# Attention and gated feed-forward: score runs of a key block in pairs, from batch 4 on

## The chip, the cores and the metric

The kernel runs on one core of a Trainium2 chip. The metric is the device time of one launch in microseconds, the median of the runs. Profiled numbers come from one execution on the same core.

## What is computed

For 8 batches of 8 heads, 576 positions and 64 dimensions: causal attention with a decay bias, then over all 4608 tokens a feed-forward layer with root-mean-square normalisation and a SiLU gate (512 to 1536 to 512).

```python
scores = scale * np.matmul(q, k.transpose(0, 1, 3, 2))
cum = np.cumsum(np.maximum(s, 0.0), axis=-1)
bias = -(cum[:, :, :, None] - cum[:, :, None, :])
scores = np.where(causal, -1e9, scores + np.minimum(bias, 0.0))
attn = softmax(scores)                     # over the keys
x = (attn @ v).transpose(0, 2, 1, 3).reshape(4608, 512)
xn = x / np.sqrt(np.mean(x * x, -1) + 1e-6) * rms_g
g = xn @ w_gate
out = (g / (1 + np.exp(-g)) * (xn @ w_val)) @ w_out
```

## The kernel before

The feed-forward runs in nine chunks of 512 tokens (`ffn`). In a chunk, for each of twelve blocks of 128 inner features, four matmuls of 128x512 make the gate (L751) and four the value (L760), each in a bank of the four-bank ring psF. ScalarE takes the tanh T of half the gate (L754), VectorE makes U = (T + 1) x gate (L763), and Ht = U x value (L756). Then four output tiles of twelve matmuls each (L773) are made; ScalarE copies them out as osb (L778).

The attention of later batches is put between these matmuls by a planner that runs while the program is written. `step()` is called 36 times in a chunk, after every block of four feed-forward matmuls or so; `slot[0]` counts the steps. The steps 1 to 24 of a chunk lie in the gate and value part, the rest among the outputs. Each step first issues what is pending from the step before, then may scale an x (`x_scale`) and start its transpose on SP's queue, run one entry of some side queues (casts, loads, magnitude checks), and then `place()` puts at most a score run, or values and transposes, into TensorE's order. A lag such as `ready(5, "S", b, qb, g)` asks that the scores were placed at least five steps ago.

Batch b has five key blocks kb; queries of a key block are the same 128 positions and the next 128. `s_step` (L249) makes the scores of one key block for four heads (g = 0 or 1): four matmuls (L278) that each use half of the rows of the array (64 dimensions), the two halves writing two banks, psS[0] and psS[1]. Four exps follow on ScalarE (L302), the first two at once and the other two in the next step, and then a mask on POOL (L311), into one of eight slots of E. The last key block has 64 positions and one run of eight small matmuls for all heads.

`av_step` (L336) makes the values of 128 queries for four heads: up to eight matmuls of 65 columns (L344, L350) into psAV for g = 0 and into psT for g = 1. VectorE takes the reciprocal of the sums (L357) and writes x_sb (L359). After g = 1, ScalarE takes the sum of squares (L366), POOL makes alpha from it (L379, L382), and `x_scale` (L389) multiplies x by alpha and the weights g_row. `xt_dma` (L400) transposes the result into xnT, which the chunks read; `need(c)` would put warm-up matmuls (L674) where a chunk's x is late.

PSUM has eight banks here: four of psF, two of psS, one of psAV, one of psT.

The rules around the change: a score run waits until the last one is 4, 3 or 2 steps back, by how far ahead of its due step it is; values until the last values are 2 steps back and their scores 5 steps; x is scaled 3 steps after the values of g = 1; the transposes of keys and queries (L182) keep off SP's queue just ahead of an x that is to be scaled. A slot of E is free when its two readers have been placed.

Of the kernel before, what the change touches and what calls it, by code (L numbers as in the profile page):

```python
# [26 lines left out]
def kernel(  # L27
# [13 lines left out]
    B, H, S, D = q.shape  # L41
# [40 lines left out]
    kqTx = kqT.rearrange("d a w (c h n) -> d a w c h n", c=NSC, h=HP)  # L82
    XB = 2
    KB = 4
    v_sb = mp.tile([128, 2, NSC, H, NV], BF16, name="v_sb")

    NE = 8
# [154 lines left out]
    def slot_free():  # L242
        return eread.get(ecount[0] % NE, 0) == 0
# [2 lines left out]
        for ps in pair:  # L246
            nc.tensor.matmul(ps, lhsT=ident_bf, rhs=mneg, start=True, stop=False)

    def s_step(b, kb, g, pair=None, masked=False):  # L249

        p = b % 2
        N = (256, 256, 256, 192, 64)[kb]
        W = 64 if kb == 4 else 256
        nj = 4 if kb == 4 else 2
        e = take_slot((b, kb, g), 2 if kb in (0, 1, 2, 3) else 2)
        if pair is None:
            ps = psS()
            pair = (ps[:, 0, :], ps[:, 1, :])

        wide, premask = b == 0, b == 0 and kb < 4  # L260
        if premask and not masked:
            masks(pair)
        heads = []
        for j in range(nj):
            hp = (0 if kb == 4 else 2 * g) + j
            for par in (0, 1):
                rs = slice(par * 64, par * 64 + 64)
                if b < KB:
                    kT = kqTn[rs, p, 0, hp, kb * 128:kb * 128 + 128]
                else:  # L270
                    kT = kqTx[rs, p, 0, kb, hp, :]
                if b < XB:
                    qT = kqTn[rs, p, 1, hp, kb * 128:kb * 128 + N]
                    M = N
                else:
                    qT = kqTx[rs, p, 1, kb, hp, 0:64] if kb == 4 else kqTx[rs, p, 1, kb:kb + 2, hp, :]
                    M = W
                nc.tensor.matmul(  # L278
                    pair[par][:, j * W:j * W + M], lhsT=kT, rhs=qT,
                    start=(j == 0 and not premask), stop=(j == nj - 1))  # L280
                heads.append((2 * hp + par, par, j * W))
        if kb == 4:
            Ev = E[:, e].rearrange("p h (a n) -> p (h a) n", n=128)
            h0, nh, nq = 0, 8, 64
        else:
            Ev = E[:, e]
            h0, nh, nq = 4 * g, 4, 128

        def exps(part):
            for h, par, o in part:  # L290
                bh = b * H + h
                parts = [(0, N)]
                if b >= XB and kb == 3:
                    parts = [(0, 128), (128, 192)]
                for n0, n1 in parts:
                    eo = Ev[:, h - h0, n0:n1]
                    ei = pair[par][:, o + n0:o + n1]
                    if b >= XB and (n1 - n0) % 128 == 0:

                        eo = eo.rearrange("k (a p r) -> k a p r", p=32, r=4)  # L300
                        ei = ei.rearrange("k (a r p) -> k a p r", p=32, r=4)
                    nc.scalar.activation(out=eo, in_=ei, func=AF.Exp, scale=0.125,  # L302
                                         bias=biasK[:, kb, bh:bh + 1])

        def second(masked=True):
            exps(heads[nj:])
            if masked:
                mask()

        def mask():  # L310
            nc.gpsimd.affine_select(  # L311
                out=Ev[:, :, 0:nq], in_=Ev[:, :, 0:nq],
                pattern=[[0, nh], [1, nq]], compare_op=ALU.is_ge, fill=0.0, base=0,
                channel_multiplier=-1)

        def whole():
            for par in (0, 1):
                nc.scalar.activation(
                    out=Ev.rearrange("k (j a) n -> k a j n", a=2)[:, par, :, 0:N],
                    in_=pair[par][:, 0:nj * W].rearrange("k (j n) -> k j n", j=nj)[:, :, 0:N],  # L320
                    func=AF.Exp, scale=0.125)

        if premask:
            return whole
        if wide:
            whole()
            return mask
        exps(heads[:nj])
        return second

# [103 lines left out]
    slot = [0]  # L434
    first, chunk = [0], [0]
    done = {}
    last = {"S": -9, "AV": -9, "T": -9, "X": -9, "AVT": -9, "L": -9}
    s_seq = [(b, kb, g) for b in range(B) for kb in range(NSC) for g in (0, 1) if kb < 4 or g == 0]
    s_seq.sort(key=lambda x: (1, 0, x[2], x[1]) if x[0] == 1 and x[1] < 2 else (x[0], x[1], x[2], 0))
    av_seq = [(b, qb, g) for b in range(B) for qb in range(NSC) for g in (0, 1)]  # L440
# [9 lines left out]
    def at(*key):  # L450
        return done.get(key, 10 ** 6)
# [30 lines left out]
    def phase():  # L482

        return slot[0] - first[0]
# [86 lines left out]
        done["T", b, hp, w] = slot[0]  # L571
        last["T"] = slot[0]

    def do_s(key, pair=None, masked=False):
        b, kb, g = key
        second = s_step(b, kb, g, pair, masked)
        done["S", b, kb, g] = slot[0]
        if kb == 4:
            done["S", b, 4, 1] = slot[0]
        last["S"] = slot[0]  # L580
        return second
# [23 lines left out]
    def can_t():  # L605
# [10 lines left out]
            return ready(2, "cast", 1, "tail") if hp == "tail" else ready(2, "cast", 1, w, hp // 2)  # L616
        return (ready(2, "cast", b) or ready(2, "cast", b, w)) and (b < 2 or ready(1, "S", b - 2, 4, 0))

    def can_s():
        if not s_seq or not slot_free():  # L620
            return False
        b, kb, g = s_seq[0]
        if b == 1 and (phase() < 24 and phase() % 2 == 0 or kb == 4 and at("AV", 1, 3, 1) > slot[0]):
            return False
        due = SLOTS * ((b * S + kb * 128) // DM) - (26 if b == 1 else 18 if b < 4 else 14)
        if slot[0] - last["S"] < (4 if slot[0] < due - 24 else 3 if slot[0] < due else 2):
            return False
        if b >= XB:
            return all(ready(5, "X", b, 1, c) for c in (kb, min(kb + 1, 4))) and (
                ready(5, "X", b, 0, kb) if b >= KB else ready(3, "T", b) if kb >= 3 else  # L630
                all(ready(3, "T", b, hp, 0) for hp in (2 * g, 2 * g + 1)))
        if kb >= 3 and not ready(3, "T", b):
            return False
        if kb == 4:
            return True
        return all(ready(3, "T", b, 2 * g + j, w) for j in (0, 1) for w in (0, 1))

    def can_av(clear=False):
        if not av_seq:
            return False  # L640
        b, qb, g = av_seq[0]
        if slot[0] - last["AV"] < (1 if (b, qb) == (1, 3) else 2):
            return False
        if b > 0 and g == 1 and slot[0] - last["T"] < 3 and not clear:
            return False
        if b > 1 and not ready(8, "V", b):
            return False
        if qb > 0 and not ready(5, "S", b, qb - 1, g):
            return False
        prev = b * NSC + qb - NX  # L650
        if prev >= 0 and at("XT", prev // NSC, prev % NSC) > slot[0]:
            return False
        return ready(4 if (b, qb) == (1, 3) else 5, "S", b, qb, g)

    def by_pe(b, qb):

# [19 lines left out]
    def step(bare=False):  # L676

        slot[0] += 1
        while pending:
            pending.pop(0)()  # L680
        moved = False
        if scaled[0] < len(x_list):
            b, qb = x_list[scaled[0]]
            if ready(3, "AV", b, qb, 1):
                x_scale(b, qb)
                scaled[0] += 1
                if not by_pe(b, qb):
                    assert xt_seq[0] == (b, qb)
                    xt_dma(*xt_seq.pop(0))
                    done["XT", b, qb] = slot[0] + 4  # L690
                    moved = True
        run_side(act_side)

        if not moved and x_seq and slot[0] - last["X"] >= 2 and not (
                scaled[0] < len(x_list) and x_list[scaled[0]] != (1, 4) and ready(1, "AV", *x_list[scaled[0]], 1)):
            b, w, c = x_seq[0]
            if (ready(1 if b == 2 else 2, "cast", b, 1) and ready(1, "S", b - 2, 4, 0)
                    and (w == 1 or ready(7, "K", b, c))):
                x_seq.pop(0)
                kq_dma(b, w, c)  # L700
                done["X", b, w, c] = last["X"] = slot[0]
                if b >= KB and (w, c) == (0, NSC - 1) and b + 2 < B:
                    casts(b + 2)
        bare = bare or chunk[0] == 0 and 30 <= phase() <= 33
        if slot[0] % 2 and not bare and not (chunk[0] == 0 and phase() >= 24):
            run_side(v_side)
        if not bare:
            run_side(pool_side)
        place()
        run_side(dve_side)  # L710

    def place():

        if can_s():
            pending.append(do_s(s_seq.pop(0)))
            if t_seq and t_seq[0][0] == 1 and can_t():
                do_t(t_seq.pop(0))
            return
# [517 lines left out]
```

## Time and profile before

| | us |
|---|---|
| Runs | 363.77, 365.58, 370.51 |
| Median | 365.58 |
| Profiled execution | 364.69 |
| Span of its profile | 363.0 |
| PE busy | 348.8 (96%) |
| VectorE (DVE) busy | 273.4 (75%) |
| ScalarE (ACT) busy | 239.8 (66%) |
| GpSimd (POOL) busy | 178.2 (49%) |

PE is TensorE's matmuls, PEld its weight loads, SP the queue of the sync engine. In the rows of the profile "L278" is a line of the kernel; a row of the timeline has the start, the time from the first start to the last end, the engine, the line, the operation, the tile written and those read, and how many instructions are merged in it. Ends of matmuls are modelled and matmuls overlap, so the order of their starts tells more than their durations. The granted clock of TensorE was 0.999 over the span.

### The profile page before, as it was taken

Reading aid. Unit: us, or ns where it says so; the run is one execution under the profiler, and the core shown is the slowest. Engines: PE = TensorE matmul, PEld = TensorE weight load, DVE = VectorE, ACT = ScalarE, POOL = GpSimd, SP = SyncE. Lnnn points to the kernel's source line nnn. Section 1 sums busy time; section 2 is a strip of 40 time slices with the busy share of each in tenths; the row PEclk is TensorE's granted clock in tenths of the full one; section 3 lists DMA queues with packets and bytes.
Section 4 is the critical chain, followed back from the end, with each engine's and each line's share of the span. In section 5 each row is a group of like instructions: output and inputs, shape, how many; then the busy total and the mean of one; then the engine's idle time right before and its main releaser. Section 6 shows DMA issues by size and latency. Waiting matters only on the chain. (4 is left out here: it accounts for less than half of the span.)

```text
span 363.0 us, 6976 instructions
## 1 busy us (share of the span) xinstructions
PE 348.8 (96%) x2383; PEld 160.5 (44%) x2383; DVE 273.4 (75%) x523; ACT 239.8 (66%) x619; POOL 178.2 (49%) x283
## 2 busy tenths in 40 slices
PE   4989999999999999999999999999999999999993
PEld 2445444444445444444444444444444444444441
DVE  6697988698888889788998988884588548827820
ACT  3988884768886778877778768776777653223311
POOL 7959765858865566869737954622232200000000
PEclk9999999999999999999999999999999999999999
DMA  7999999999969399969979994973201130020011
GB/s 228 132 229 256 177 170 259 182 201 193 212 127 138 59 198 138 167 147 163 164 202 124 140 142 105 115 85 90 78 14 17 51 103 1 0 88 29 1 60 60
DMA packets 124096, 45.81 MB, mean 126 GB/s; under 512 B 103956, under 2 KB 118808, under 8 KB 124056
## 3 DMA queue, kind: packets, MB, share of 16 engines
q0 software_dynamic: 62688, 14.29, 47.4%
q1 hardware_dynamic: 51872, 23.80, 32.1%
q10 hardware_dynamic: 9496, 7.23, 8.4%
q8 instruction: 19, 0.31, 0.4%
q14 instruction: 21, 0.17, 0.2%
HBM read 37.90 MB, written 9.44 MB: 130 GB/s over the span
## 5 line engine op out<-in xcount | busy, mean ns | idle before, releaser
L302 ACT ACTIVATE E<-psS,biasK 128x256 bf16<-128x256 f32 (+3 forms) x328 | 107.0, 415 | 18.9 <-PE psS L278 18.6
L751 PE MATMUL psF<-xnT,wg_sb 128*128 128x512 bf16 x432 | 111.1, 379 | 0.6 <-ACT xnT L416 0.3
L760 PE MATMUL psF<-xnT,wv_sb 128*128 128x512 bf16 x432 | 111.1, 379 | 0.0
L773 PE MATMUL psF<-wout_sb,Ht 128*128 128x512 bf16 x432 | 102.5, 379 | 0.1
L763 DVE SCALAR_TENSOR_TENSOR U<-T,psF 128x512 bf16<-128x512 f32 x108 | 73.7, 682 | 29.4 <-ACT T L754 29.4
L754 ACT ACTIVATE T<-psF 128x512 f32<-128x512 f32 x108 | 64.4, 596 | 41.0 <-PE psF L751 38.6
L311 POOL TENSOR_SCALAR_AFFINE_SELECT E<-E 128x512 bf16<-128x512 bf16 x64 | 46.5, 727 | 77.5 <-ACT E L302 77.0
L756 DVE TENSOR_TENSOR Ht<-U,psF 128x512 bf16<-128x512 bf16 x99 | 67.7, 684 | 7.0 <-PE psF L760 0.5
L751 PEld LDWEIGHTS <-wg_sb 128*128 128x128 bf16 x432 | 38.7, 98 | 44.9 <-issue 5.6
L773 PEld LDWEIGHTS <-Ht 128*128 128x128 bf16 x432 | 38.6, 97 | 42.4 <-issue 2.3
L760 PEld LDWEIGHTS <-wv_sb 128*128 128x128 bf16 x432 | 38.5, 98 | 42.2 <-issue 4.2
L778 ACT ACTIVATE osb<-psF 128x512 f32<-128x512 f32 x36 | 21.5, 596 | 32.0 <-PE psF L773 25.5
L389 DVE SCALAR_TENSOR_TENSOR xs_sb<-x_sb,al_all,g_row 128x512 bf16<-128x512 bf16 (+1 forms) x36 | 29.9, 831 | 12.8 <-POOL al_all L382 12.1
L186 POOL DMA_DIRECT2D v_sb<-in_v_dram x40 | 35.4, 888 | 0.7 <-PE psAV L350 0.3
L366 ACT ACTIVATE xs_sb<-x_sb 128x512 bf16<-128x512 bf16 (+1 forms) x37 | 23.5, 636 | 17.9 <-DVE x_sb L359 17.5
L427 DVE TENSOR_TENSOR acc<-acc,mag 128x1280 bf16<-128x1280 bf16 x32 | 26.6, 845 | 0.2
L278 PE MATMUL psS<-kqT 64*128 64x256 bf16 (+2 forms) x304 | 25.9, 256 | 0.9 <-ACT kqT L203 0.5
L350 PEld LDWEIGHTS <-E 128*128 128x128 bf16 x320 | 21.7, 98 | 10.0 <-issue 0.2
L379 POOL TENSOR_SCALAR al_all<-ss_all 128x1 f32<-128x1 f32 (+2 forms) x39 | 10.7, 274 | 29.7 <-ACT xs_sb L366 22.9
L382 POOL TENSOR_TENSOR al_all<-al_all,mhalf 128x1 f32<-128x1 f32 (+2 forms) x39 | 22.2, 570 | 3.2
L344 PEld LDWEIGHTS <-E 128*128 128x128 bf16 x256 | 20.0, 98 | 8.6 <-DVE x_sb L359 1.6
L278 PEld LDWEIGHTS <-kqT 64*128 64x128 bf16 x320 | 9.2, 94 | 30.8 <-issue 29.9
(126 smaller groups left out, 301.0 us busy)
## 6 DMA issues: line engine op xcount, KB each, us to landing
out_dram<-osb SPq DMA_DIRECT2D x36, 256.0 KB, 2.3
kq<-in_q_dram ACTq DMA_DIRECT2D x5, 1024.0 KB, 6.2
v_sb<-in_v_dram POOLq DMA_DIRECT2D x32, 128.0 KB, 6.4
kq<-in_k_dram SPq DMA_DIRECT2D x4, 512.0 KB, 5.6
kq<-in_q_dram SPq DMA_DIRECT2D x4, 512.0 KB, 7.5
kqn<-in_k_dram POOLq DMA_DIRECT2D x16, 128.0 KB, 5.4
wout_sb<-in_moe_w_out_dram POOLq DMA_DIRECT2D x2, 768.0 KB, 9.9
kq<-in_q_dram POOLq DMA_DIRECT2D x1, 1024.0 KB, 10.8
```

Of the source, the lines that this page charges most:

```text
L186: nc.gpsimd.dma_start(out=v_sb[0:n, b % 2, c, :, 0:64], in_=v[b, :, c * 128:c * 128 + n, :].rearrange("h p d -> p h d"))
L278: nc.tensor.matmul(pair[par][:, j * W:j * W + M], lhsT=kT, rhs=qT, start=(j == 0 and not premask), stop=(j == nj - 1))
L302: nc.scalar.activation(out=eo, in_=ei, func=AF.Exp, scale=0.125, bias=biasK[:, kb, bh:bh + 1])
L311: nc.gpsimd.affine_select(out=Ev[:, :, 0:nq], in_=Ev[:, :, 0:nq], pattern=[[0, nh], [1, nq]], compare_op=ALU.is_ge, fill=0.0, base=0, chan ...
L389: nc.vector.scalar_tensor_tensor(out=xs_sb[0:n, (b * NSC + qb) % NX, :], in0=x_sb[0:n, (b * NSC + qb) % NX, :], scalar=al_all[0:n, col:col ...
L427: nc.vector.tensor_tensor(out=acc[:, sl], in0=acc[:, sl], in1=mag[:, sl], op=ALU.max)
L751: nc.tensor.matmul(Gp, lhsT=wg_sb[:, cc, fs], rhs=xnT[:, cc, x0:x0 + DM], start=(cc == 0), stop=(cc == CC - 1))
L754: nc.scalar.activation(out=T, in_=Gp, func=AF.Tanh, scale=0.5)
L756: nc.vector.tensor_tensor(out=Ht[:, fb - 1, :], in0=pend[0], in1=pend[1], op=ALU.mult)
L760: nc.tensor.matmul(Vp, lhsT=wv_sb[:, cc, fs], rhs=xnT[:, cc, x0:x0 + DM], start=(cc == 0), stop=(cc == CC - 1))
L763: nc.vector.scalar_tensor_tensor(out=U, in0=T, scalar=1.0, in1=Gp, op0=ALU.add, op1=ALU.mult)
L773: nc.tensor.matmul(Op, lhsT=Ht[:, fb, tb * 128:(tb + 1) * 128], rhs=wout_sb[:, fb, :], start=(fb == 0), stop=(fb == FB - 1))
```

## The change

From batch 4 on (`PB = 4`), and for the four large key blocks, `place()` takes both score runs of a key block in one step. The run of g = 1 comes first and goes to psS; its exps are held. The run of g = 0 follows at once and goes to psAV and psT, the banks of the values. The exps of g = 0 are issued in this step and the next one, those of g = 1 in the two steps after that, so `pending` now holds a step for each entry. A pair waits for the last scores (six steps after the held run, which is counted two steps late; four steps at the first key block), for the last values (two steps) and for two free slots of E; values wait three steps after a pair, since they use its banks. The values of g = 1 may follow those of g = 0 in the next step, four steps after their scores' counted step. From batch 4 on x is scaled five steps behind its values instead of three, and the transposes on SP keep off accordingly. Score runs that are not paired wait three steps from batch 4 on.

```diff
+    PB = 4
...
-    def s_step(b, kb, g, pair=None, masked=False):
+    def s_step(b, kb, g, pair=None, masked=False, hold=False):
...
+        if hold:
+            return lambda: exps(heads[:nj]), second
         exps(heads[:nj])
         return second
...
-    last = {"S": -9, "AV": -9, "T": -9, "X": -9, "AVT": -9, "L": -9}
+    last = {"P": -9, "S": -9, "AV": -9, "T": -9, "X": -9, "AVT": -9, "L": -9}
...
-    def do_s(key, pair=None, masked=False):
+    def do_s(key, pair=None, masked=False, hold=False):
         b, kb, g = key
-        second = s_step(b, kb, g, pair, masked)
+        second = s_step(b, kb, g, pair, masked, hold)
...
+    def paired(key):
+        return key[0] >= PB and key[1] < 4 and key[2] == 0
+
     def can_s():
-        if not s_seq or not slot_free():
+        if not s_seq or not slot_free() or pending:
             return False
         b, kb, g = s_seq[0]
+        if paired(s_seq[0]):
+            if eread.get((ecount[0] + 1) % NE, 0) > 0 or slot[0] - last["AV"] < 2:
+                return False
+            if slot[0] - last["S"] < (6 if kb else 4):
+                return False
...
-        if slot[0] - last["S"] < (4 if slot[0] < due - 24 else 3 if slot[0] < due else 2):
+        if slot[0] - last["S"] < (3 if b >= PB else 4 if slot[0] < due - 24 else 3 if slot[0] < due else 2):
             return False
...
-        if slot[0] - last["AV"] < (1 if (b, qb) == (1, 3) else 2):
+        if slot[0] - last["AV"] < (1 if (b, qb) == (1, 3) or b >= PB and g == 1 else 2):
+            return False
+        if slot[0] - last["P"] < 3:
             return False
...
-        return ready(4 if (b, qb) == (1, 3) else 5, "S", b, qb, g)
+        return ready(4 if (b, qb) == (1, 3) or b >= PB and g == 1 and qb < 4 else 5, "S", b, qb, g)
...
-        while pending:
-            pending.pop(0)()
+        while pending and pending[0][0] <= slot[0]:
+            pending.pop(0)[1]()
...
-            if ready(3, "AV", b, qb, 1):
+            if ready(3 if b < PB else 5, "AV", b, qb, 1):
                 x_scale(b, qb)
...
-                scaled[0] < len(x_list) and x_list[scaled[0]] != (1, 4) and ready(1, "AV", *x_list[scaled[0]], 1)):
+                scaled[0] < len(x_list) and x_list[scaled[0]] != (1, 4) and ready(1 if x_list[scaled[0]][0] < PB else 3, "AV", *x_list[scaled[0]], 1)):
...
         if can_s():
-            pending.append(do_s(s_seq.pop(0)))
+            if paired(s_seq[0]):
+
+                b, kb, g = s_seq.pop(0)
+                first4, last4 = do_s(s_seq.pop(0), hold=True)
+                pair = (psAV(), psT32())
+                pending.extend([(slot[0] + 1, do_s((b, kb, g), pair)),
+                                (slot[0] + 2, first4), (slot[0] + 3, last4)])
+                done["S", b, kb, 1] = slot[0] + 2
+                last["P"], last["S"] = slot[0], slot[0] + 2
+                return
+            pending.append((slot[0] + 1, do_s(s_seq.pop(0))))
```

## The prediction

> **What bounds the kernel now.** I read the page first (busy times, the 40 slices), then the windows of the part in which batches 4 to 7 are scored, then the groups of lines there, then the order of TensorE's work in single steps.
>
> ```profile
> span 363.0 us, 6976 instructions
> PE 348.8 (96%) x2383; PEld 160.5 (44%) x2383; DVE 273.4 (75%) x523; ACT 239.8 (66%) x619; POOL 178.2 (49%) x283
> PE   4989999999999999999999999999999999999993
> ```
>
> ```profile
> 143.50:179.00 35.50, 35.50 (x258) 16.07 (x256) 29.91 (x56) 27.24 (x80) 28.21 (x44) 1.00 1.49 154
> 179.00:214.00 35.00, 35.00 (x248) 15.66 (x247) 31.84 (x61) 26.80 (x75) 22.59 (x35) 1.00 1.32 154
> 214.00:250.00 36.00, 36.00 (x253) 16.14 (x252) 29.46 (x55) 26.32 (x72) 14.89 (x24) 1.00 0.80 104
> 250.00:286.00 36.00, 36.00 (x253) 16.17 (x252) 24.23 (x47) 26.11 (x72) 9.96 (x19) 1.00 0.17 47
> ```
>
> After the stretch's length the columns are PE, PEld, DVE, ACT and POOL busy, the granted clock and DMA. TensorE never idles between 143.5 and 286 us; no other engine is full (DVE at most 31.84 of 35.00). So nothing that only takes load off another engine shortens this part. What can shorten it is time in which TensorE counts as busy and streams nothing. I looked for that around a score run (four score matmuls):
>
> ```profile
> 201.31 1.03 PE L760 MATMUL psF<-xnT,wv_sb 128*128 128x512 bf16 x4
> 202.27 0.39 PE L278 MATMUL psS<-kqT 64*128 64x256 bf16 x4
> 202.60 1.04 PE L751 MATMUL psF<-xnT,wg_sb 128*128 128x512 bf16 x4
> 203.47 0.19 PE L344 MATMUL psT<-v_sb,E 128*128 128x65 bf16 x1
> ...
> 203.71 1.02 PE L760 MATMUL psF<-xnT,wv_sb 128*128 128x512 bf16 x4
> 204.57 1.03 PE L751 MATMUL psF<-xnT,wg_sb 128*128 128x512 bf16 x4
> 205.44 1.03 PE L760 MATMUL psF<-xnT,wv_sb 128*128 128x512 bf16 x4
> ```
>
> ```profile
> L278 PE MATMUL psS<-kqT x304: 190/269/280, 10.5 to 284.7; 64*128 64x256 bf16 x114, 64*128 64x64 bf16 x32, 64*128 64x192 bf16 x6
> ```
>
> Start to start, an undisturbed feed-forward block of four takes 0.86 to 0.87 us (203.71, 204.57, 205.44); I use 0.865. The block before the scores takes 0.96 (201.31 to 202.27), the scores 0.33, the block behind 0.87. A score run therefore costs 0.96 + 0.33 + 0.87 - 2 x 0.865 = **0.43 us**. Inside it little time is streaming: the four records span 0.39 us and one lasts 0.27, so the last starts 0.12 after the first; the two pairs (one matmul on each half of the rows) follow each other at 0.12. Two pairs are 0.24; the other 0.19 is the price of going from full-height matmuls to half-height ones and back.
>
> **The change, part by part.**
>
> *Pairing the score runs.* Batches 4 to 7, key blocks 0 to 3: 16 pairs of runs. Two runs apart cost 0.86. Eight matmuls in a row cost 0.43 + 2 x 0.12 = 0.67, so a pair saves 0.19 and 16 save **3.0 us**. The second four write psAV and psT, which no score run of the trace does, so I bound them: at least the pace of the feed-forward, 512 columns in 0.865/4 = 0.216 us (then 0.21 saved each, 3.4 in all); at most a whole run of 0.43 again (nothing saved). I take 0.24, since they are the same shape behind the same shape, as the second pair of a run is now.
>
> By the Trainium skill (TensorEngine Tiling (Array Packing), Tiling Modes, Key Properties) the array drains when the tiling mode changes and not when only the tile does, which is for 0.24 rather than 0.43; no run here has two score runs in a row.
>
> *The step pattern.* From the rules: pair at step k, its values at k+5 and k+6, the next pair at k+8 (the held run counts as k+2, plus six; the values plus two). By hand the pairs fall on steps 109, 119, 127, 135, 144, 153, 161, 169, 178, 187, 195, 203, 212, 221, 229, 237: about 34 steps for a batch, where the feed-forward supplies 36 x 576/512 = 40.5. Scores end at step 242, the last scaling at 253, of 324 steps; chunk 4, starting at step 144, needs a block scaled at 130, that is 14 x 0.865 = 12 us earlier. So attention is never late for a chunk:
>
> ```profile
> DMA to landing us min/median/max: 2.3/3.7/8.5
> L400 SPq DMA_TRANSPOSE xnT<-xs_sb x34: 1171/1190/1852, 56.5 to 295.5; - x34
> 325.31 1.03 PE L751 MATMUL psF<-xnT,wg_sb 128*128 128x512 bf16 x4
> ```
>
> The last transpose is issued at 295.5 and the last chunk begins at 325.31. Scaling two steps later (1.7 us) costs nothing by this cover; without it, 1.7 us per chunk. SP's queue holds the same transposes, and each waits less for its scaling; the loads keep their order on POOL.
>
> *The exps.* A run's exps now occupy two steps; a pair's occupy four in a row, with the tanhs between, on ScalarE's one queue. Rows for the durations:
>
> ```profile
> 200.04 0.83 ACT L302 ACTIVATE E<-psS,biasK 128x256 bf16<-128x256 f32 x2
> 201.21 0.90 POOL L162 DMA_DIRECT2D kqn<-in_k_dram  x1
> 202.71 1.03 ACT L302 ACTIVATE E<-psS,biasK 128x128 bf16<-128x128 f32 x4 [0.60 <-PE psS L278]
> 203.67 0.60 ACT L754 ACTIVATE T<-psF 128x512 f32<-128x512 f32 x1
> 204.06 0.18 DVE L357 RECIPROCAL rZ<-psT 128x4 f32<-128x4 f32 x1
> 204.16 1.03 ACT L302 ACTIVATE E<-psS,biasK 128x128 bf16<-128x128 f32 x4
> 204.27 0.42 DVE L359 TENSOR_TENSOR x_sb<-psT,rZ 128x256 bf16<-128x256 f32 x1
> 204.61 0.68 DVE L763 SCALAR_TENSOR_TENSOR U<-T,psF 128x512 bf16<-128x512 f32 x1
> 205.06 0.63 POOL L311 TENSOR_SCALAR_AFFINE_SELECT E<-E 128x512 bf16<-128x512 bf16 x1
> 205.64 0.60 POOL L156 CAST kqn<-kq 128x512 bf16<-128x512 f32 x1
> ...
> 207.60 0.19 PE L344 MATMUL psAV<-v_sb,E 128*128 128x65 bf16 x1
> ```
>
> Neighbours on ScalarE overlap by some 0.08 (the exps of 202.71 end at 203.74, the tanh starts at 203.67), so two exps occupy 0.75; a tanh occupies 0.49 (203.67 to 204.16) and starts 0.20 after its block (203.47). Let a pair's first matmul start at 0, in the gate/value part, behind a gate block. TensorE: scores to 0.57, then blocks to 1.44, 2.30, 3.17, 4.03, 4.90; the first values 4.90 to 5.14; a block; the second values at 6.00. ScalarE: exps start 0.44 after the scores (202.27 to 202.71) plus 0.24 = 0.68; the first half-runs end at 1.43 and 2.18; a tanh 2.50 to 3.0; the held half-runs end at 3.75 and 4.50; the next tanh, due at 4.23, starts at 4.50. Its gate bank is wanted only two blocks after the one that follows it, so this delay of 0.27 is hidden.
>
> POOL's masks (0.63) end at 2.8 and 5.1. The first values want theirs at 4.90, the second at 6.00: **0.9 us of cover**, where a run has 1.9 today (scores 202.27, mask over at 205.69, values 207.60). Queued ahead of the held mask are the key and value issues (0.90 each): from 2.8, two of them end at 4.6 and the mask at 5.2, still in time; with a cast (0.60) too the mask ends at 5.8. A mask can also last longer:
>
> ```profile
> L311 POOL TENSOR_SCALAR_AFFINE_SELECT E<-E x64: 624/635/1331, 30.9 to 287.4; 128x512 bf16<-128x512 bf16 x64
> L389 DVE SCALAR_TENSOR_TENSOR xs_sb<-x_sb,al_all,g_row x36: 732/752/1428, 42.2 to 294.1; 128x512 bf16<-128x512 bf16 x28, 64x512 bf16<-64x512 bf16 x8
> ```
>
> The longest took 1.33, 0.70 over the median. In the new order the scaling of x (step k+3 when pairs are eight apart) is issued in the same step as the held mask. With 0.70 more, behind three issues, the mask ends at 6.5: a wait of 0.5. I count one such case in 16, about 0.3 us with smaller ones. Lower bound 0; upper bound every pair, in the rival below.
>
> The Trainium skill (SBUF — State Buffer, Who interferes with whom) has a rule that speaks against the move: a VectorE instruction with two inputs in SBUF and a GpSimd one that reads SBUF exclude each other for a whole instruction. The two maxima above agree in size; by it alone, every pair with a scaling in its mask's step would see that delay, yet only those also behind three issues would wait.
>
> *The banks psAV and psT.* The second four wait for VectorE's reads of the values two steps earlier. These end 0.98 after the values (203.71 to 204.69), so at 6.24 + 0.98 = 7.2; with one Ht or U (0.68) ahead, 7.9. The next pair's second four start at 0.57 + 8 x 0.865 + 2 x 0.24 + 0.10 + 0.24 = 8.3. Covered by 0.4. If it fails, the next thing late is the whole row of eight matmuls and TensorE with it.
>
> **Sum.** The profiled execution took 364.69 us (span 363.0 and 1.69 around it). 364.69 - 3.0 + 0.3 = **362.0 us**. The profiled execution lies 0.89 below the median of the runs shown (365.58), and the fastest run 0.92 below the profiled one (363.77); 362.0 is 1.0% under the median.
>
> **The rivals.**
>
> 1. *Small waits eat half.* VectorE is at 31.84 of 35.00 in its fullest window, so the cover of 0.4 on the banks can fail where pairs follow eight steps apart in the gate/value part. Six do (127, 161, 195, 203, 229, 237); at 0.3 each 1.8 us: 363.5. Against it: the scaling no longer waits for alpha there.
> 2. *The switch is paid again* for the second four because they go to other banks: nothing saved, 364.7. Against it: pairs inside a run already alternate between two banks at 0.12.
> 3. *The held half's mask decides* (slower). If exps do not overlap (0.83 a half-run, tanh 0.60), the held half ends at 0.68 + 1.66 + 0.17 + 0.60 + 1.66 = 4.8; with one issue of 0.90 after that, the mask ends at 6.3, and at 7.0 where it lasts 1.33. TensorE then waits some 0.75 (between 0.3 and 1.0) at the second values. In the 11 pairs of the gate/value part this is 8.3: 364.69 - 3.0 + 8.3 = 370.0. It decides from 0.19 per pair on, a held mask that ends 1.1 us later than I have it. For it: today too POOL waits for exps before anything else. Against it: POOL is busy only 9.96 to 28.21 of some 36 us, and the overlap is in the rows.
>
> **How the numbers follow.** Forecast 0.58 (its own range 361.0 to 363.0), rival 1 0.22, rival 2 0.05, rival 3 0.12, something larger in either direction 0.03. The range goes down to 360.3 (3.4 saved, no waits, and the 0.9 by which the fastest run is under the profiled one) and up to 367.0, which leaves out most of rival 3. A difference under 2% is about what a measurement of this kernel can't tell from none. Faster by over 2% would take 7.3 us, more than twice all that the switches of these runs cost: 0.03. Slower by over 2% means 373 us, rival 3 in every pair: 0.05. Within: 0.92.
>
> **What would show it.** Right: in the changed profile score runs of eight, about 0.57 from first start to the next block; eight steps between them; values in neighbouring steps; PE still full between 143 and 283, that stretch some 3 us shorter; masks of held runs ending before their values. Wrong: idle time of PEld or PE before L344/L350 put to POOL (rival 3) or before L278 put to VectorE (rival 1); a gap of 0.2 inside the row of eight (rival 2); warm-up matmuls (L674) between chunks, which would mean that x came late.

## The result and the profile after

The changed kernel takes 367.45 us (median of 22 runs, 366.21 to 371.65), the kernel before 365.84 (22 runs). The ratio is 1.0063, 95% interval 1.0038 to 1.0088: a small loss, where 362.0, a gain of 1%, was forecast and 367.0 was the upper end of the range. The profiled executions took 366.71 and 364.69, with spans of 365.0 and 363.0.

The change does what it says. In the order of TensorE's work there are score runs of eight, the second four in psAV and psT (the columns are start, time to the last end, engine, line):

```profile
200.40 1.03 PE L783 MATMUL psF<-xnT,wv_sb 128*128 128x512 bf16 x4
201.35 0.39 PE L279 MATMUL psS<-kqT 64*128 64x256 bf16 x4
201.58 0.27 PE L279 MATMUL psAV<-kqT 64*128 64x256 bf16 x1
201.59 0.27 PE L279 MATMUL psT<-kqT 64*128 64x256 bf16 x1
201.69 0.27 PE L279 MATMUL psAV<-kqT 64*128 64x256 bf16 x1
201.69 0.27 PE L279 MATMUL psT<-kqT 64*128 64x256 bf16 x1
201.90 1.04 PE L774 MATMUL psF<-xnT,wg_sb 128*128 128x512 bf16 x4
202.77 1.03 PE L783 MATMUL psF<-xnT,wv_sb 128*128 128x512 bf16 x4
```

The block before the scores takes 0.95, the eight matmuls 0.55, the block behind 0.87; against two undisturbed blocks (1.73) a pair costs 0.64, where two single runs cost 0.86. Each pair saves 0.21 to 0.22 us, 16 save 3.4.

What was lost shows in the busy times of the scored part, 145 to 290 us, before and after (columns: stretch, PE, PEld, DVE, ACT, POOL busy, clock, DMA share, GB/s):

```profile
145.00:290.00 145.00, 145.00 (x1018) 65.17 (x1016) 115.73 (x219) 107.72 (x297) 76.19 (x122) 1.00 0.91 113
```

```profile
145.00:290.00 145.00, 142.29 (x1013) 67.60 (x1012) 115.00 (x218) 106.50 (x299) 76.95 (x122) 1.00 0.94 113
```

TensorE, full before, now idles 2.71 us. A matmul's record runs on for some 0.16 us after the next could start (0.38 long, at a pace of 0.216), so a gap that the profile calls idle is that much longer from start to start. I sum the gaps between starts beyond the undisturbed pace: **4.45 us**, against 0 before. They are twelve gaps: 2.6 in front of values (five), 1.0 in front of the small run of the last key block (four, the largest 0.62), 0.5 inside rows of eight (two) and 0.3 in front of a value block. The list of waits of this stretch (who waits, for whom, us in total, times, longest) names the releasers:

```profile
PEld L353 <- POOL E L312: 3.3, 5, 1.0
PE psT L353 <- POOL E L312: 1.5, 3, 0.7
PE psS L279 <- ACT E L303: 0.6, 1, 0.6
PEld L279 <- DVE x_sb L362: 0.5, 2, 0.3
```

The masks on POOL come first. The small run waits for ScalarE's exps, which read psS; the rows of eight for VectorE's x_sb, which reads psAV and psT. So 3.4 saved and 4.45 waited make the changed part 1.0 us longer. Of the other 1.0 us between the profiled spans, 0.7 is a wait for x in chunk 1:

```profile
69.19 1.04 PE L774 MATMUL psF<-xnT,wg_sb 128*128 128x512 bf16 x4 [0.97 <-DMA xnT<-xs_sb]
```

```profile
68.41 1.04 PE L751 MATMUL psF<-xnT,wg_sb 128*128 128x512 bf16 x4 [0.23 <-DVE rZ L357]
```

The first row is the changed kernel's, the second that of the kernel before; from start to start the gaps are 1.13 and 0.39. There the order of the instructions is still that of before (the planner's choices differ from step 108 on), and the same gap was between nothing and 1.9 us long in the executions profiled later, so this is the executions' own variation. The last 0.3 is not accounted for.

### The profile page after: what moved, and what is told of

Read it like the earlier page. It is cut to its first block, busy times and chain, and to the rows that moved or that the text cites. A ratio compares the mean times of both kernels' runs of the same rounds, so it can differ in the third digit from the quotient of the medians.

```text
span 365.0 us, 6948 instructions
## 1 busy us (share of the span) xinstructions
PE 347.2 (95%) x2383; PEld 163.6 (45%) x2383; DVE 273.0 (75%) x523; ACT 238.6 (65%) x619; POOL 179.2 (49%) x283
## 5 line engine op out<-in xcount | busy, mean ns | idle before, releaser
L303 ACT ACTIVATE E<-psS,biasK 128x256 bf16<-128x256 f32 (+3 forms) x248 | 79.9, 426 | 3.2 <-PE psS L279 3.1
L312 POOL TENSOR_SCALAR_AFFINE_SELECT E<-E 128x512 bf16<-128x512 bf16 x64 | 45.6, 714 | 60.3 <-ACT E L303 60.0
L392 DVE SCALAR_TENSOR_TENSOR xs_sb<-x_sb,al_all,g_row 128x512 bf16<-128x512 bf16 (+1 forms) x36 | 29.0, 805 | 6.7 <-POOL al_all L385 6.0
L430 DVE TENSOR_TENSOR acc<-acc,mag 128x1280 bf16<-128x1280 bf16 x32 | 27.4, 870 | 0.3
L385 POOL TENSOR_TENSOR al_all<-al_all,mhalf 128x1 f32<-128x1 f32 (+2 forms) x39 | 23.8, 609 | 3.2
L279 PEld LDWEIGHTS <-kqT 64*128 64x128 bf16 x320 | 10.9, 94 | 25.5 <-issue 23.7
L279 PE MATMUL psS<-kqT 64*128 64x256 bf16 (+2 forms) x240 | 19.6, 250 | 1.6 <-ACT E L303 0.9
```

Of the source, the lines that this page charges most:

```text
L279: nc.tensor.matmul(pair[par][:, j * W:j * W + M], lhsT=kT, rhs=qT, start=(j == 0 and not premask), stop=(j == nj - 1))
L312: nc.gpsimd.affine_select(out=Ev[:, :, 0:nq], in_=Ev[:, :, 0:nq], pattern=[[0, nh], [1, nq]], compare_op=ALU.is_ge, fill=0.0, base=0, chan ...
L392: nc.vector.scalar_tensor_tensor(out=xs_sb[0:n, (b * NSC + qb) % NX, :], in0=x_sb[0:n, (b * NSC + qb) % NX, :], scalar=al_all[0:n, col:col ...
L430: nc.vector.tensor_tensor(out=acc[:, sl], in0=acc[:, sl], in1=mag[:, sl], op=ALU.max)
```

## Experiments

Theory P: POOL is full where key and value loads are issued, and masks queue behind the issues. Theory S: ScalarE's Square stands in front of a tanh and the pair's exps while it waits for x_sb, so everything behind is late. Both name a queue in front of the masks. "Gaps" in the table is the sum from start to start between 145 and 290 us, as above, and "behind" what lies behind 290 us and not in the kernel before too; the ratio is to the kernel before, with its interval.

| kernel | median us | ratio (95%) | gaps us | behind us |
|---|---|---|---|---|
| changed kernel | 367.45 | 1.0063 (1.0038 to 1.0088) | 4.45 | 0 |
| Square a step later | 366.05 | 0.9990 (0.9962 to 1.0018) | 3.69 | 0 |
| quiet steps behind a pair | 363.62 | 0.9938 (0.9911 to 0.9965) | 1.48 | 0 |
| the same, second time | 363.75 | 0.9946 (0.9922 to 0.9969) | 1.64 | 0 |
| pairs at odd steps | 365.94 | 0.9986 (0.9955 to 1.0018) | 3.27 | 0 |
| later scaling alone | 365.64 | 0.9979 (0.9953 to 1.0005) | 0 | 0 |
| held masks left out | 366.11 | 1.0000 (0.9965 to 1.0035) | 3.25 | 0 |
| x scaled after three steps | 366.43 | 1.0011 (0.9984 to 1.0039) | 3.51 | 0 |
| pair three steps after values | 365.40 | 0.9976 (0.9945 to 1.0008) | 2.26 | 1.5 |
| quiet, three steps, small run later | 364.82 | 0.9967 (0.9937 to 0.9998) | 0.68 | 1.5 |
| spread loads | 364.71 | 0.9964 (0.9932 to 0.9995) | 2.95 | 0 |
| spread, odd | 363.61 | 0.9945 (0.9925 to 0.9965) | 1.50 | 0 |
| spread, odd, small run later | 362.76 | 0.9917 (0.9886 to 0.9947) | 0 | 0.3 |

**Square a step later.**

```diff
         if g == 1 and not apart:
-            norm()
+            if b < PB:
+                norm()
+            else:
+                late.append((slot[0] + 1, norm))
...
         slot[0] += 1
+        while late and late[0][0] <= slot[0]:
+            late.pop(0)[1]()
```

> The changed kernel with the sum of squares (ScalarE, Square) and the alpha behind it issued one step later, from batch 4 on. In the changed kernel TensorE waits 4.45 us in its scored part (145 to 290 us), of which 2.6 in front of values for masks, 1.0 in front of the small score run, 0.5 inside rows of eight and 0.3 in front of a value block. Theory S (ScalarE's order: Square waits for x_sb in front of a tanh and of the pair's exps): most of these go, under 1.5 us is left, about 364 us. Theory P (POOL's load issues stand ahead of the held mask): the waits for masks stay above 2 us, the total above 3.5, about 366.5 us.

Gaps of 3.69, of which 2.4 are still in front of values (0.85, 0.41, 0.22, 0.10, 0.86). The waits for masks hardly shrink, and the total stays above 3.5, as theory P has it; the other gaps shrink by 0.6. (In the profiled execution of this kernel the scored part lies 6 us later, at full clock, and the gaps are summed there.)

**Quiet steps behind a pair.**

```diff
         bare = bare or chunk[0] == 0 and 30 <= phase() <= 33
+        bare = bare or 1 <= slot[0] - last["P"] <= 2
```

> The changed kernel with no entry of the loads' and casts' queues in the two steps behind a pair, so that nothing of them stands between the two masks of a pair on POOL. Theory P: the 2.6 us of waits for masks fall under 0.6, the other 1.8 us stay, about 364.5 us. Theory S: the masks stay late because their exps are late, the waits for masks stay above 1.5 us, about 366 us.

No gap is left in front of values, and the kernel beats the one before by 0.5 to 0.6%, in two runs of the experiment. But more changed than the queue: the delayed loads also moved pairs from even to odd steps of the gate/value part. The next experiment has those steps without the quiet.

**Pairs at odd steps.**

```diff
-            if slot[0] - last["S"] < (6 if kb else 4):
+            if slot[0] - last["S"] < (6 if kb else 4) or phase() < 24 and phase() % 2 == 0:
                 return False
```

> The changed kernel with pairs in the gate/value part only at odd steps, behind a gate block (steps 127, 135, 144, 153, ..., as the prediction had them by hand; the changed kernel has most of them at even steps, behind a value block). Theory S: the values of g = 1 then come behind a gate block whose tanh is already issued, so Square holds up one tanh less; the waits fall from 4.45 to under 2 us, about 364 us. Theory P: nothing about the loads changes, the waits for masks stay above 2 us, about 366.5 us.

Gaps of 3.27, 1.75 of them at masks (a later expectation says 1.9, with a gap right behind the values). The 1.75 are a little under the 2 that theory P asked for, and the total is far over the 2 of theory S. One gap is 1.4 us alone:

```profile
208.13 0.19 PE L347 MATMUL psT<-v_sb,E 128*128 128x65 bf16 x1
209.57 0.20 PE L353 MATMUL psT<-v_sb,E 128*128 128x65 bf16 x1 [1.25 <-POOL E L312]
```

From step 157 on TensorE's order is the same in this kernel and the quiet one, with pairs at 161, 169, 178 and so on. Of the 1.75 at masks 1.6 lie there, and the quiet steps take them to 0. That is theory P without the confusion. The place of the pairs is worth 1.2 of its own.

**Later scaling alone.**

```diff
-            if ready(3, "AV", b, qb, 1):
+            if ready(3 if b < PB else 5, "AV", b, qb, 1):
...
-                ... ready(1, "AV", *x_list[scaled[0]], 1)):
+                ... ready(1 if x_list[scaled[0]][0] < PB else 3, "AV", *x_list[scaled[0]], 1)):
```

> The kernel before with only x scaled five steps behind its values from batch 4 on; no pairs. Both theories: the scaling is off TensorE's path, no waits appear between 145 and 290 us, and the time is that of the kernel before within 0.3%. If the later scaling were a cause of the loss, TensorE would wait here too.

No gap in the scored part, and no difference in time: the scaling is off the path by itself.

**Held masks left out.**

```diff
-            if masked:
+            if masked and not (hold and b >= PB):
                 mask()
```

> The changed kernel without the masks of the held runs (16 masks on POOL are left out, so half of the heads of batches 4 to 7 see later keys of their own block). Theory P: the values of g = 1 then wait for exps only, which end in time, so the waits of 0.47, 0.66, 0.27 and 0.87 us in front of them (2.3 of 4.45) go to under 0.3; the waits in front of small runs and inside rows of eight stay, about 364.5 us. Theory S: the exps themselves are late, over 1 us of these waits stays, about 366 us.

This kernel leaves out 16 masks that the result needs; it serves for its times alone. The gaps in front of values are gone, all of them, so the masks and not the exps were what ended them (without the 16, POOL also has that much less to do). Yet 3.25 us remain, since TensorE now waits more at other places: rows of eight 1.2 (0.5 in the changed kernel), small runs 1.5 (1.0 there).

```profile
PEld L279 <- DVE x_sb L362: 1.2, 2, 0.7
PE psS L279 <- ACT E L303: 1.0, 2, 0.6
PE psT L279 <- DVE x_sb L362: 0.6, 2, 0.4
```

**x scaled after three steps**, the pairs kept.

```diff
-            if ready(3 if b < PB else 5, "AV", b, qb, 1):
+            if ready(3, "AV", b, qb, 1):
```

(The condition that keeps SP's transposes off is set back as well.)

> The changed kernel with x scaled three steps behind its values everywhere, as before. If the later scaling helped VectorE, which reads the banks that the pairs write, the waits inside rows of eight grow from 0.5 us to over 1.5 and the time by 1 us or more; if it is of no weight, waits and time are those of the changed kernel within 1 us (4.45, 367.5).

Gaps of 3.51, 0.7 of them inside rows of eight: neither the 1.5 nor the growth that would have made the later scaling a help. It may even cost the pairs something: the mask gaps are 0.9 us in three here, against 2.6 in five, and the ratio is 1.0011 against 1.0063. That fits the scaling not being issued beside a mask. But the key loads, too, are issued at other steps here, and 0.8 us of gaps in front of feed-forward blocks (0.3 in the changed kernel) take a part back, so the share of the scaling is not separated.

**Pair three steps after the values.**

```diff
-            ... or slot[0] - last["AV"] < 2:
+            ... or slot[0] - last["AV"] < 3:
```

> The changed kernel with a pair three steps behind the last values instead of two, so nine steps between pairs. Theory D (VectorE is late with x_sb, so the banks psAV and psT are late): the waits inside rows of eight go, which are only 0.5 us here. By theory P a step more also lets POOL and ScalarE catch up between pairs, so waits for masks shrink by perhaps half, from 2.6 to 1.3; total 2 to 2.5 us, about 365 us. If POOL's order inside the pair alone decides, the waits for masks stay above 2 us.

The rows of eight have no gap left, and the masks one of 0.45, which fits POOL catching up where pairs are nine or more steps apart. The small runs still cost 1.2, 0.4 is a wait for x at the start of chunk 4 and 0.2 one in front of a gate block. Attention now lasts into chunk 7, where 0.6 us are lost in front of feed-forward blocks and 0.9 at the last small run. So 365.4 is near the 365 expected, though the sum is made of other parts.

**Quiet, three steps, small run later.** On top of both edits:

```diff
-        if slot[0] - last["S"] < (3 if b >= PB else ...):
+        if slot[0] - last["S"] < (4 if b >= PB and kb == 4 else 3 if b >= PB else ...):
```

> The kernel with the quiet two steps behind a pair, and on top a pair three steps behind the last values and the small run (last key block) four steps behind the held run's counted step instead of three. The quiet steps alone left 1.48 us of waits: 1.07 inside a row of eight (VectorE), 0.27 in front of small runs, 0.14 in front of a gate block. If these causes are right, under 0.3 us of waits is left and the time is 1.2 us under the quiet kernel, about 362.4 us against 366 of before.

0.68 in the scored part, 0.57 of it at masks again in spite of the quiet steps, and 1.5 behind it, in chunk 7, where VectorE also reduces acc (L836 of the kernel before). A miss: 362.4 was expected, and the ratio of 0.9967 is no better than the 0.9938 of the quiet kernel alone, though the intervals overlap. More distance between pairs is not the remedy.

**Spread loads.** The pairs stay at the steps of the changed kernel; only the key loads wait until the value loads are issued.

```diff
-            pool_side.extend((lambda: free(0) and slot[0] % 2 == 0, ...
+            pool_side.extend((lambda: free(0) and slot[0] % 2 == 0 and not (b > 5 and v_side), ...
```

> The changed kernel with its pairs at the same steps, and the key loads of batches 6 and 7 held back until the value loads issued on the same queue are out, so that POOL gets one load issue in two steps instead of one in each. In the changed kernel POOL is busy 8.34 of 8.50 us (163.0 to 171.5) and 11.64 of 11.80 (196.7 to 208.5), where the waits for masks are. Theory P (POOL is full there and the masks queue behind issues): the 2.6 us of waits for masks fall under 0.8, the total under 2.8, about 365.3 us. Theory S (exps late behind Square): the waits for masks stay above 1.5 us.

The expectation quotes these rows of the changed kernel, where POOL (the fifth busy time) has no time left:

```profile
163.00:171.50 8.50, 8.19 (x58) 3.83 (x56) 7.19 (x15) 5.90 (x14) 8.34 (x13) 1.00 2.26 160
196.70:208.50 11.80, 10.89 (x76) 4.94 (x74) 10.50 (x21) 7.63 (x19) 11.64 (x17) 1.00 1.68 116
```

With the loads spread, a single gap of 0.06 is left in front of values, though 2.95 remain in all, a little over the 2.8 expected (rows of eight 1.0, small runs 1.6, a value block 0.3). Theory P is shown with the order of TensorE unchanged. It holds for the casts of the loaded keys, too, which the edit moves along with the loads. The five gaps of the changed kernel lie at 170.94, 181.26, 199.31, 206.62 and 208.60, and the second, of 0.66, has no load issue ahead of its mask. There casts fill the queue, and two masks take 1.21 and 1.22 where most take 0.63 (the second is the first half of the last row):

```profile
176.09 1.62 POOL L157 CAST kqn<-kq 128x512 bf16<-128x512 f32 x2
177.68 1.21 POOL L312 TENSOR_SCALAR_AFFINE_SELECT E<-E 128x512 bf16<-128x512 bf16 x1
178.84 1.19 POOL L146 CAST kqn<-kq 128x512 bf16<-128x512 f32 x1
179.99 1.83 POOL L312 TENSOR_SCALAR_AFFINE_SELECT E<-E 128x512 bf16<-128x512 bf16 x2
```

The kernel gains 0.0099 in ratio on the changed one, each against the kernel before beside it. That is 3.6 us, of which the gaps of the two profiled executions show 1.5 (4.45 to 2.95); the rest is not accounted for. What is left in the scored part is mostly the other two waits, and they have grown: at the row of eight behind the first of the five gaps 0.47 + 0.21 became 0 + 0.71, since its bank waits for VectorE's x_sb, whenever TensorE comes.

**Spread and odd steps; and the small run a step later** (the edits above put together).

> The spread key loads and in addition pairs only at odd steps of the gate/value part. Odd steps alone left 3.27 us of waits, 1.9 of them for masks and 0.87 in front of small runs. If POOL's load and the place of the pairs are two causes that add up: under 1.5 us of waits, about 364 us, as with the quiet steps (363.6 against 366.3 of before). If the spread does nothing where pairs stand at odd steps, 3 us of waits and 366 us.

> The kernel with spread loads and odd steps, and the small run a step later. The waits in front of small runs (0.87 us at odd steps alone) go; everything else as with spread and odd steps; 0.5 us less than that kernel, about 363.5 us, if the extra steps bring no attention into the stretch of chunk 7 in which VectorE also reduces acc (there 1.5 us were lost with pairs nine steps apart).

1.50 us of gaps with two edits, none with three. Against pairs at odd steps alone, the first of these kernels has the same order on TensorE and only the loads spread: the 1.75 at masks go to 0 once more. The third edit also moves some pairs to ten steps apart, so it is not the small run alone that took away the 0.5 inside a row of eight. The best kernel is full again in the scored part:

```profile
145.00:290.00 145.00, 145.00 (x1034) 69.28 (x1032) 114.74 (x217) 106.63 (x299) 75.94 (x120) 1.00 0.88 116
```

Its span is 361.1 us, and it takes 362.76 against 365.54 of the kernel before beside it, 0.9917 (0.9886 to 0.9947). It beats the kernel before, and by these ratios the changed one.

> The kernel with the quiet two steps once more, beside the spread loads on one chip, to see whether it beats the kernel before: ratio about 0.994, waits 1.2 to 1.8 us; if its first result was luck of the runs, the ratio is 0.998 or more.

The quiet kernel's first result held.

## Why the prediction was wrong

**Right: the saving.** A pair costs 0.64 where 0.67 was forecast, and the second four in other banks follow at the feed-forward's pace (0.23 behind the first, 201.35 to 201.58), near the lower bound given. 3.4 saved where 3.0 stood in the sum; the kernel without gaps in the scored part shows most of it, 2.8 us by the medians. Rival 2 is out.

**Wrong: the waits, 0.3 in the sum and 4.45 on the chip.** Four steps failed.

The step on POOL failed most. The prediction started POOL empty at the first mask and counted only the issues between the two masks, and it set rival 3 aside by POOL's busy time over some 36 us. Shorter windows of the kernel before (the fifth busy time is POOL's) show it full there already:

```profile
163.00:171.50 8.50, 8.50 (x59) 3.81 (x58) 7.61 (x16) 6.04 (x18) 8.30 (x12) 1.00 2.25 162
200.00:206.00 6.00, 6.00 (x38) 2.71 (x37) 5.62 (x12) 4.76 (x16) 5.92 (x9) 1.00 2.03 138
```

So the prediction's reading that no engine but TensorE is full was an average over too long a stretch. In the changed kernel, for the pair at 201.35:

```profile
200.07 0.88 POOL L163 DMA_DIRECT2D kqn<-in_k_dram  x1
200.94 0.89 POOL L187 DMA_DIRECT2D v_sb<-in_v_dram  x1
201.80 0.90 POOL L163 DMA_DIRECT2D kqn<-in_k_dram  x1
202.78 0.19 POOL L382 TENSOR_SCALAR al_all<-ss_all 128x1 f32<-128x1 f32 x1
203.04 0.56 POOL L385 TENSOR_TENSOR al_all<-al_all,mhalf 128x1 f32<-128x1 f32 x1
203.57 0.96 POOL L187 DMA_DIRECT2D v_sb<-in_v_dram  x1
204.52 0.89 POOL L163 DMA_DIRECT2D kqn<-in_k_dram  x1
205.40 1.16 POOL L312 TENSOR_SCALAR_AFFINE_SELECT E<-E 128x512 bf16<-128x512 bf16 x1
206.52 0.69 POOL L187 DMA_DIRECT2D v_sb<-in_v_dram  x1
207.19 0.70 POOL L163 DMA_DIRECT2D kqn<-in_k_dram  x1
207.88 0.67 POOL L312 TENSOR_SCALAR_AFFINE_SELECT E<-E 128x512 bf16<-128x512 bf16 x1
```

An issue of 0.9 in every step of 0.865 fills POOL by itself; two masks and alpha in eight steps come on top. The first mask starts 4.05 after the scores (2.2 forecast) and the held one at 6.5 and ends at 7.2 (5.1 to 5.8 forecast). The values at 206.22 and 207.70 wait. The exps of the two halves are late too, but less:

```profile
203.95 0.50 ACT L303 ACTIVATE E<-psT,biasK 128x256 bf16<-128x256 f32 x1
205.50 0.90 ACT L303 ACTIVATE E<-psS,biasK 128x256 bf16<-128x256 f32 x2
```

They end 3.10 and 5.05 after the scores (2.18 and 4.50 forecast), so about half of the first mask's delay is theirs, and the held mask starts 1.5 after the last of its exps. A like load lay on POOL before, but a mask then had 1.9 us of cover; the change cut it to 0.9 by holding half of the exps. It was rival 3's place with another mechanism: less the slow exps than a queue full for two batches' loads, so 2.6 us in five gaps and not 8.3 in eleven.

The planner by hand was wrong. It had the pairs of the gate/value part at odd steps (127, 153, 161, 187, ...); but for the first two, the changed kernel has them at 126, 152, 160, 186, 194, 202, 220, 228 and 236, behind a value block. There the exps meet Square first:

```profile
201.30 0.63 ACT L369 ACTIVATE xs_sb<-x_sb 128x512 bf16<-128x512 bf16 x1 [2.60 <-DVE x_sb L362]
201.84 0.19 ACT L369 ACTIVATION_READ_ACCUMULATOR xs_sb<-x_sb 128x1 f32 x1
201.93 0.58 ACT L777 ACTIVATE T<-psF 128x512 f32<-128x512 f32 x1
202.41 0.47 ACT L303 ACTIVATE E<-psAV,biasK 128x256 bf16<-128x256 f32 x1
```

The exps start 1.06 after the scores instead of 0.68. Square a step later wins back 0.8 us of the gaps, pairs at odd steps 1.2; theory S was a part, not the whole.

The small run (last key block) was not in the sum at all. Its bank psS is free only after the held exps; the prediction followed psAV and psT and not the bank from which the exps were delayed. It cost 1.0 us.

The banks' cover of 0.4 failed in two rows of eight for 0.5 us (rival 1 gave 1.8 for six). The 0.3 in front of a value block was in no step of the prediction; the gap is gone where Square comes a step later, which points to ScalarE's order but does not prove it.

The point on the scaling was right where it stands alone: it costs nothing in the kernel before, and x came late for no chunk behind step 108. Beside the pairs that is not shown, as the run with three steps says. Where it runs beside a mask it can lengthen it, as weighed:

```profile
205.32 0.74 DVE L392 SCALAR_TENSOR_TENSOR xs_sb<-x_sb,al_all,g_row 128x512 bf16<-128x512 bf16 x1
```

The mask of 205.40 took 1.16 while the scaling ran from 205.32 to 206.06; the next mask took 0.67. The rule of the Trainium skill that was weighed there (SBUF — State Buffer, Who interferes with whom: such a pair of instructions excludes each other) agrees with this row. It is the only mask of the scored part that is longer than 0.7 us beside a scaling, and by my estimate about 0.5 of the 1.2 us that TensorE waits at this pair: the held mask stands 0.5 later in the queue for it. So the one case in 16 for which the sum had its 0.3 did come; the other 2.1 us at masks were not in the sum.

Three smaller points of the prediction do not hold. Behind three issues of 0.90 its long mask would end at 6.8; 6.5 is two issues and a cast. The parts of the range's lower end give 360.4 and not 360.3. And differences far under the 2% that it took for the limit can be told from none: the intervals here reach 0.2 to 0.35% to either side.

## What to carry to other kernels

A queue that is half idle on average can be full for the length of a few steps, and what counts for a moved instruction is the queue at its own step: start the sum from the work already queued, and compare the demand of a cycle with its length. When work is held back, list every buffer that it keeps occupied and who wants it next. Removing one wait shows the next, so causes are to be taken away together before a restructuring is called a loss: the same pairing went from 0.6% slower to 0.8% faster with three small edits to the planner's rules.

## What the runs showed of the hardware

A row of eight half-height matmuls that writes four banks keeps the pace of a run of four that writes two (0.11 to 0.12 for a pair of 256 columns each: 201.35, 201.58, 201.69, and 0.55 for eight where four took 0.33). The change between full-height and half-height matmuls costs about 0.2 us per run, there and back (0.43 for a run of which 0.24 is streaming). A load issued from POOL occupies that engine for 0.69 to 0.96 us in the rows above, in order with its masks.
